# Zones of a one-core attention and MoE kernel, each 64 bytes longer

## The chip, the core and the metric

The kernel runs on one core of a Trainium2 chip. Its time is the device time of one execution in microseconds (us). Three runs of the kernel before took 904.09, 905.15 and 905.59 us; the median is 905.15 us. TensorE is the matrix engine (PE in the profile, PEld its loading of weights), VectorE is DVE, ScalarE is ACT, GpSimd is POOL, SyncE is SP. SBUF is the on-chip memory of 128 partitions that all operands are read from; PSUM holds the matmuls' results.

## The reference

Attention in four batches of eight heads, 576 positions, head size 64: half of the heads see a local window of 32 positions, half every 32nd position. Its output x (2304 tokens x 512) goes through two gated layers:

```
x = concat_heads(softmax(mask(q @ k.T / 8)) @ v)        # 2304 x 512
x = ((x @ w_a) * (x @ w_b)) @ w_out                     # 512 -> 1536 -> 512
y = (sigmoid(x @ w_gate) * (x @ w_val)) @ w_out2        # 512 -> 1536 -> 512
```

## The kernel before

Each fp32 product of the two layers is made of three passes over a high and a low part of both operands (high x high, low x high, high x low), in the type fp32r. The work has three stages.

**Stage one** (to about 502 us) holds the attention and the first layer. Tokens come in five tiles, four of 512 tokens and one of 256. For each tile and each of the 12 blocks k of 128 features, TensorE does 2 x 12 matmuls for the two factors (line 923, helper `product`) and 12 for the output of the block before (line 1013, `first_output`). The attention of the next tile is laid between these: the score products at line 563 (`qk`), the products with the values at line 618, transposes at lines 604 and 877. VectorE does the strided heads by multiplying and summing (lines 781 to 851).

**Stage two** (to about 770 us) is the gate and the value of the second layer, and **stage three** its output matrix. Both form block products with seven instead of eight multiplications: `seven` builds products whose matmuls, all at line 1292 (`prod`), have 384 columns. A product has 6 matmuls in stage two (two halves of the contraction, three passes) and 18 in stage three. Stage two runs 18 groups of two times 7 products, stage three 3 times two times 7. VectorE forms sums (`combine`, line 1133), splits operands (`split`, line 1144, with ScalarE at 1142) and merges results (lines 1304 and 1375).

The order of all work is made by a planner (`Plan`): each operation has an engine, a cost, a due time and the ranges of memory that it touches, and `run` issues the operation that can start first. Ranges are given in one flat address space in units of four bytes. It begins with 17 zones (`REGIONS`): 12 of 3072 elements (w0 to w11, 12288 bytes in each partition), four of 2048 (x12 to x15) and one of 1024 (h16). In stage one a w zone holds one block k's three weights in two parts, the x zones hold the tokens and h16 the features between the two products of the layer. In stages two and three the same zones hold tokens, weights, sums and their parts in other shares. What follows the zones (work buffers, raw weights, the ring of the attention) lies in one tile named `rest`.

The function `at(a, n, phase)` turns a flat range into a view of a tile. A zone's tile is made when the zone is first asked for in a phase, and all phases of a zone share one place in SBUF, since they have one tag:

```
if tiles.get(r, (None,))[0] != phase:
    name = f"{('w', 'x', 'h')[(r[0] >= X0) + (r[0] >= H0)]}{REGIONS.index(r)}"
    tiles[r] = phase, sb.tile([P, r[1]], F32, tag=name, name=f"{name}p{phase}")
v = tiles[r][1][:, a - r[0]:a - r[0] + n]
```

Tiles are laid behind each other in the order in which their tags are first used: the identity, the mask, `rest` (which begins at a multiple of 512 bytes), two small ones, then the zones w11, w10, w9, w7, w6, w8, w5, four small tiles of together 512 bytes, w4, x12, x14, x13, x15, w0, w1, h16, w2, w3. With "line" for a piece of 64 bytes, counted modulo 512 bytes (lines 0 to 7), every zone of the kernel before begins on line 6, and the 17 zones end at byte 228224 of a partition. Weights, tokens, features and their parts begin at multiples of 512 bytes from their zone's beginning: a block of weights is 128 columns of 4 bytes, a moving operand is 256, 384 or 512 such columns.

Of the kernel before, what the change touches and what calls it, by code (L numbers as in the profile page):

```python
# [7 lines left out]
F32 = mybir.dt.float32  # L8
# [14 lines left out]
P = 128  # L23
# [54 lines left out]
for _n, (_k, _w) in RINGS.items():  # L78
    if _n not in PLACE:
        PLACE[_n] = TOP  # L80
        TOP += _k * _w


def region_of(a):
    return next((r for r in REGIONS if r[0] <= a < r[0] + r[1]), None)
# [260 lines left out]
def attention_moe_kernel(ctx, tc, qkv, sq, sk, sv, w1, w2, mask, ident, out):  # L346
# [4 lines left out]
    sb = ctx.enter_context(tc.tile_pool(name="sb", bufs=1))  # L351
# [10 lines left out]
    tiles = {}  # L362

    def at(a, n, phase=FIRST, dtype=F32):
        r = region_of(a)
        if r is None:
            v = rest[:, a - F0:a - F0 + n]
        else:
            if tiles.get(r, (None,))[0] != phase:
                name = f"{('w', 'x', 'h')[(r[0] >= X0) + (r[0] >= H0)]}{REGIONS.index(r)}"  # L370
                tiles[r] = phase, sb.tile([P, r[1]], F32, tag=name, name=f"{name}p{phase}")
            v = tiles[r][1][:, a - r[0]:a - r[0] + n]
        return v if dtype == F32 else v.bitcast(dtype)

    def xT(i, c):

        return at(X0 + (2 * i + c // 2) * XZONE, XZONE, FIRST, F32R).rearrange("p (c n) -> p c n", c=HK)
# [5 lines left out]
    def buf(op, ring, shape, dtype=F32):  # L383
        s = op.slot[ring][0]
        if ring in PLACE:
            return at(PLACE[ring] + s * RINGS[ring][1], shape[1], FIRST, dtype)
        return sb.tile(shape, dtype, tag=f"{ring}{s}", name=f"{ring}{s}")
# [65 lines left out]
    def convert(w, need, start=()):  # L453
# [3 lines left out]
        def clear(op):  # L457
            for i in op.slot["c"]:
                tops.append(at(PLACE["c"] + i * DM, DM, FIRST, U32))
                POOL.memset(tops[-1], 0)  # L460
# [1133 lines left out]
```

## Time and profile before

| what | before |
|---|---|
| median of three runs | 905.15 us (904.09 to 905.59) |
| the profiled execution's own time | 903.51 us |
| its span, first to last instruction | 901.7 us |
| instructions in the profile | 13664 |
| TensorE busy | 893.2 us, 99% |
| VectorE, ScalarE, GpSimd busy | 654.9, 405.7, 11.7 us |

The profiled execution takes 1.8 us more than its span, and 1.6 us less than the median. The page gives the busy time of each engine, the chain of work that ended last, followed back from the last instruction, and the costliest groups of instructions; other views give the chain in order of time, the waits, stretches of time, or one line's instructions. A matmul's duration in the trace (334 ns for 384 columns) is longer than the distance to the next one's start, since matmuls are pipelined; what counts for the time is the distance, the pitch. It is read from the chain in order of time, where a piece gives its start, its length and the number of instructions in it.

### The profile page before, as it was taken

Reading aid. Unit: us, or ns where it says so; the run is one execution under the profiler, and the core shown is the slowest. Engines: PE = TensorE matmul, PEld = TensorE weight load, DVE = VectorE, ACT = ScalarE, POOL = GpSimd, SP = SyncE. Lnnn points to the kernel's source line nnn. Section 1 sums busy time; section 2 is a strip of 40 time slices with the busy share of each in tenths; the row PEclk is TensorE's granted clock in tenths of the full one; section 3 lists DMA queues with packets and bytes.
Section 4 is the critical chain, followed back from the end, with each engine's and each line's share of the span. In section 5 each row is a group of like instructions: output and inputs, shape, how many; then the busy total and the mean of one; then the engine's idle time right before and its main releaser. Section 6 shows DMA issues by size and latency. Waiting matters only on the chain.

```text
span 901.7 us, 13664 instructions
## 1 busy us (share of the span) xinstructions
PE 893.2 (99%) x5170; PEld 802.6 (89%) x5170; DVE 654.9 (73%) x1078; ACT 405.7 (45%) x843; POOL 11.7 (1%) x23
## 2 busy tenths in 40 slices
PE   8999999999999999999999999999999999999998
PEld 4678888888888888888899999999999999999998
DVE  7999988998999878811328876675768458649491
ACT  5775644411242113311236655564666445435351
POOL 4000000000000000000000000000000000000000
PEclk9999999999999999999999999999999999999999
DMA  9666564312332124300035243645574588953501
GB/s 311 203 232 219 201 201 135 91 44 63 92 128 72 54 65 144 96 1 1 0 118 164 94 139 113 216 152 187 200 243 168 196 306 331 378 166 116 167 17 62
DMA packets 62513, 132.67 MB, mean 147 GB/s; under 512 B 5872, under 2 KB 37232, under 8 KB 61552
## 3 DMA queue, kind: packets, MB, share of 16 engines
q1 hardware_dynamic: 62160, 131.60, 43.9%
q8 instruction: 40, 0.66, 0.3%
q10 hardware_dynamic: 288, 0.21, 0.1%
q14 instruction: 25, 0.20, 0.1%
HBM read 97.19 MB, written 34.60 MB: 146 GB/s over the span
## 4 chain that ended last, share of the span: by engine, by line
PE 96%; DVE 3%; DMA 0%; ACT 0%; issue 0%; DVEq 0%
PE bank L1292 43%; PE bank L923 32%; PE bank L1013 16%; PE idle L423 1%; PE bank L563 1%; PE bank L618 1%; PE bank L604 1%; DMA rest<-w 0%; PE bank L877 0%; DVE rest L491 0%; PE bank L436 0%; DVE w8p L851 0%; DVE w9p L851 0%; DVE nm L575 0%; DVE x14p L630 0%
## 5 line engine op out<-in xcount | busy, mean ns | idle before, releaser
L947 ACT CAST h16p<-rest 128x512 fp32r<-128x512 f32 (+1 forms) x60 | 34.7, 579 | 144.1 <-PE bank L1013 140.1
L1304 DVE TENSOR_TENSOR rest<-bank,rest 128x384 f32<-128x384 f32 x84 | 46.4, 555 | 57.3 <-PE bank L1292 32.5
L943 DVE TENSOR_TENSOR rest<-bank,rest 128x512 f32<-128x512 f32 (+1 forms) x60 | 38.1, 635 | 54.4 <-PE bank L923 54.1
L1065 ACT COPY rest<-bank 128x512 f32<-128x512 f32 (+1 forms) x60 | 32.7, 545 | 93.1 <-PE bank L923 91.6
L1310 ACT COPY rest<-bank 128x384 f32<-128x384 f32 x84 | 40.1, 479 | 67.2 <-PE bank L1292 66.9
L951 DVE TENSOR_TENSOR h16p<-rest,h16p 128x512 fp32r<-128x512 f32 (+1 forms) x60 | 38.2, 636 | 29.1 <-PE bank L1013 23.6
L781 DVE TENSOR_TENSOR rest<-rest 128x320 f32<-128x320 f32 (+13 forms) x56 | 51.5, 920 | 1.3 <-DMA rest<-sq 0.5
L844 DVE TENSOR_TENSOR rest<-rest,s 128x320 f32<-128x320 f32 (+13 forms) x56 | 51.5, 920 | 0.9
L787 DVE TENSOR_REDUCE s<-rest 128x5 f32<-128x320 f32 (+13 forms) x56 | 51.2, 914 | 1.2
L851 DVE TENSOR_REDUCE rest<-rest 128x64 f32<-128x320 f32 (+13 forms) x56 | 51.2, 914 | 1.0
L482 ACT ACTIVATE rest<-rest 128x512 f16<-128x512 bf16 x36 | 28.4, 793 | 9.2 <-DMA rest<-w 9.1
L1202 DVE SCALAR_TENSOR_TENSOR rest<-rest 128x512 uint32<-128x512 uint32 x36 | 24.7, 688 | 10.2 <-ACT rest L1195 10.2
L1195 ACT ACTIVATE rest<-rest 128x512 f16<-128x512 bf16 x36 | 28.0, 790 | 5.9 <-DMA rest<-w 5.8
L1375 DVE TENSOR_TENSOR rest<-bank,rest 128x384 f32<-128x384 f32 x36 | 20.0, 557 | 11.8 <-PE bank L1292 11.0
L1314 ACT COPY bank<-bank 128x384 f32<-128x384 f32 x42 | 19.6, 467 | 18.6 <-PE bank L1292 18.2
L1369 ACT ACTIVATE rest<-bank 128x384 f32<-128x384 f32 x36 | 17.8, 493 | 21.4 <-PE bank L1292 21.2
L491 DVE SCALAR_TENSOR_TENSOR rest<-rest 128x512 uint32<-128x512 uint32 x36 | 24.5, 684 | 0.9 <-ACT rest L482 0.9
L581 ACT ACTIVATE rest<-bank,nm 128x96 f32<-128x96 f32 x56 | 18.3, 339 | 12.2 <-DVE nm L576 10.6
L1369 ACT ACTIVATE rest<-rest 128x768 f32<-128x768 f32 x18 | 15.2, 846 | 14.2 <-DVE rest L1304 13.8
L1292 PE MATMUL bank<-w8p,w10p 128*128 128x384 f32 x100 | 20.7, 334 | 0.0
L1375 DVE TENSOR_TENSOR rest<-rest 128x768 f32<-128x768 f32 x18 | 17.2, 953 | 0.7 <-ACT rest L1369 0.2
L1292 PEld LDWEIGHTS bank<-w8p,w10p 128*128 128x128 f32 x100 | 17.6, 188 | 0.0
(500 smaller groups left out, 2413.8 us busy)
## 6 DMA issues: line engine op xcount, KB each, us to landing
rest<-w SPq DMA_DIRECT2D x72, 511.8 KB, 4.2
h2d<-rest SPq DMA_DIRECT2D x18, 768.0 KB, 4.2
rest<-qkv SPq DMA_DIRECT2D x12, 416.0 KB, 4.2
w2p<-h2d SPq DMA_DIRECT2D x12, 384.0 KB, 5.5
w0p<-h2d SPq DMA_DIRECT2D x12, 384.0 KB, 5.5
w1p<-h2d SPq DMA_DIRECT2D x12, 384.0 KB, 5.5
out<-rest SPq DMA_DIRECT2D x24, 192.0 KB, 1.8
x2d<-rest SPq DMA_DIRECT2D x16, 256.0 KB, 2.1
```

Of the source, the lines that this page charges most:

```text
L781: engine[op.eng].tensor_tensor(out=product(op, n), in0=x["k", h][:, :, :n, :], in1=x["q"][h // 2][:, e:e + nh, j:j + 1, :].to_broadcast([P ...
L787: DVE.tensor_reduce(out=weights_of(h, j, n), in_=x["p", op.deps[0]], op=ALU.add, axis=AX.X)
L844: engine[op.eng].tensor_tensor(out=product(op, n, "p (h d t) -> p h d t"), in0=x["v", h][:, :, :, :n], in1=weights_of(h, j, n).unsqueeze(2 ...
L851: DVE.tensor_reduce(out=xs[:, j, e:e + nh, :], in_=x["p", op.deps[0]], op=ALU.add, axis=AX.X)
L923: PE.matmul(x[tag][:, :n], ww[:, c * P:(c + 1) * P], xx(c), start=(u == 0 and c == chunks[0]), stop=(u == last and c == chunks[-1]),)
L943: DVE.tensor_tensor(out=x["g"], in0=x["b"][:, :n], in1=x["g"], op=ALU.mult)
L951: DVE.tensor_tensor(out=x["hl"], in0=x["g"], in1=r32(x["hh"]), op=ALU.subtract)
L1013: PE.matmul(ps[:, :n], ww[:, m * P:(m + 1) * P], x[xx], start=start, stop=stop)
L1292: PE.matmul(bank_of(where), at(*lhs(a, (0, 1, 0)[q], c), F32R), at(*rhs(b, (0, 0, 1)[q], c), F32R), start=p in OPENS and (q, c) == units[0 ...
L1304: DVE.tensor_tensor(out=at(*o), in0=bank_of("Z"), in1=at(*a), op=ALU.add)
L1310: "ACT", act2(NS), lambda op: ACT.copy(out=at(*o), in_=bank_of("Y")), [ops[after]], key - 20))
L1375: DVE.tensor_tensor(out=at(*o), in0=src(), in1=at(*o), op=ALU.mult)
```

## The change

Each zone's tile is 16 elements (64 bytes) longer, those of x12, x13 and x14 excepted. The views into the tiles stay as they were, at the tile's beginning. Since the tiles lie behind each other, each zone after a longer one begins 64 bytes further on; the zones end at byte 229120.

```
@@ -79,6 +79,9 @@
     if _n not in PLACE:
         PLACE[_n] = TOP
         TOP += _k * _w
+
+
+LINE, SAME = 16, ("x12", "x13", "x14")
 
 
 def region_of(a):
@@ -368,7 +371,7 @@
         else:
             if tiles.get(r, (None,))[0] != phase:
                 name = f"{('w', 'x', 'h')[(r[0] >= X0) + (r[0] >= H0)]}{REGIONS.index(r)}"
-                tiles[r] = phase, sb.tile([P, r[1]], F32, tag=name, name=f"{name}p{phase}")
+                tiles[r] = phase, sb.tile([P, r[1] + LINE * (name not in SAME)], F32, tag=name, name=f"{name}p{phase}")
             v = tiles[r][1][:, a - r[0]:a - r[0] + n]
         return v if dtype == F32 else v.bitcast(dtype)
```

## Rows read from the trace of the kernel before

**Rows 1.** The page: busy us and share of each engine; the granted clock in tenths

```profile
PE 893.2 (99%) x5170; PEld 802.6 (89%) x5170; DVE 654.9 (73%) x1078; ACT 405.7 (45%) x843; POOL 11.7 (1%) x23
...
PEclk9999999999999999999999999999999999999999
```

**Rows 2.** The page: the chain that ended last, shares by engine and by line

```profile
PE 96%; DVE 3%; DMA 0%; ACT 0%; issue 0%; DVEq 0%
PE bank L1292 43%; PE bank L923 32%; PE bank L1013 16%; PE idle L423 1%; PE bank L563 1%; PE bank L618 1%; PE bank L604 1%; DMA rest<-w 0%; PE bank L877 0%; DVE rest L491 0%; PE bank L436 0%; DVE w8p L851 0%; DVE w9p L851 0%; DVE nm L575 0%; DVE x14p L630 0%
```

**Rows 3.** Waits of TensorE: who waited for whom, us in total, times, longest

```profile
PE idle L423 <- DVE nil L421: 1.0, 1, 1.0
PE bank L877 <- DVE w9p L851: 0.8, 1, 0.8
PE bank L923 <- ACT x12p L627: 0.6, 1, 0.6
PE bank L1292 <- DVE w4p L1248: 0.6, 1, 0.6
```

**Rows 4.** The chain in order of time: start us, length us, what, how many

```profile
5.78 3.67 PE idle L423 x17
...
38.34 4.33 DMA rest<-w
...
106.85 2.72 PE bank L923 x12
...
458.22 2.88 PE bank L923 x24
...
503.58 43.69 PE bank L1292 x252
552.12 346.28 PE bank L1292 x1996
```

**Rows 5.** Stretches, line 1292 alone: PE and PEld busy (count), clock, DMA share, GB/s

```profile
720.00:740.00 20.00, 20.00 (x118) 20.00 (x117) 1.00 0.85 290
...
860.00:880.00 20.00, 20.00 (x117) 20.00 (x116) 1.00 0.03 11
```

**Rows 6.** The chain in order of time: the attention's score products at line 563

```profile
150.56 0.47 PE bank L563 x16
...
161.40 0.47 PE bank L563 x16
...
173.14 0.47 PE bank L563 x16
```

**Rows 7.** The chain in order of time: after transposes, and after 256-column matmuls

```profile
110.01 2.77 PE bank L923 x12
...
451.16 2.75 PE bank L1013 x12
```

**Rows 8.** Line 1292, 552.2 to 560 us: weight loads, duration ns min/median/max, starts

```profile
L1292 PEld LDWEIGHTS bank<-w1p,w10p x12: 188/188/188, 555.9 to 559.9; 128*128 128x128 f32 x12
...
L1292 PEld LDWEIGHTS bank<-w2p,w4p x10: 186/188/189, 552.1 to 554.7; 128*128 128x128 f32 x10
```

**Rows 9.** VectorE groups of 768 columns: count, busy us, mean ns, idle before

```profile
L1375 DVE TENSOR_TENSOR rest<-rest 128x768 f32<-128x768 f32 x18 | 17.2, 953 | 0.7 <-ACT rest L1369 0.2
...
L1133 DVE TENSOR_TENSOR rest<-w2p,rest 128x768 f32<-128x768 f32 x12 | 11.2, 950 | 0.0
L1133 DVE TENSOR_TENSOR rest<-w1p,w0p 128x768 f32<-128x768 f32 x9 | 8.4, 953 | 0.3 <-DMA w1p<-h2d 0.3
```

**Rows 10.** The page: DMA issues, KB each, median us to landing

```profile
rest<-qkv SPq DMA_DIRECT2D x12, 416.0 KB, 4.2
w2p<-h2d SPq DMA_DIRECT2D x12, 384.0 KB, 5.5
```

More of the change, by code (lines that the diff above doesn't have):

```diff
@@ L81 @@
         TOP += _k * _w
+LINE, SAME = 16, ("x12", "x13", "x14")
 def region_of(a):
@@ L370, in at @@
                 name = f"{('w', 'x', 'h')[(r[0] >= X0) + (r[0] >= H0)]}{REGIONS.index(r)}"
-                tiles[r] = phase, sb.tile([P, r[1]], F32, tag=name, name=f"{name}p{phase}")
+                tiles[r] = phase, sb.tile([P, r[1] + LINE * (name not in SAME)], F32, tag=name, name=f"{name}p{phase}")
             v = tiles[r][1][:, a - r[0]:a - r[0] + n]
```

## The prediction

> **What bounds the kernel now.** I read the profile from the outside in. The page's busy times [rows 1] show TensorE busy for 893.2 of 901.7 us at a granted clock of 1.0, that is 2.4 GHz, in all 40 slices; the reader should see that no other engine comes near it (VectorE 73%). Busy time alone does not say that TensorE sets the end, so the second view is the chain that ended last [rows 2]: 96% of it is TensorE, 43%, 32% and 16% in the lines 1292, 923 and 1013. The third is the table of waits [rows 3]: the longest single wait of TensorE is 1.0 us, at the start, and the largest totals are about 1 us. So from about 48 us to the end TensorE runs one matmul after the other, and the time is a count of matmuls times their pitch (start to start).
>
> The pitch is in the chain's long pieces [rows 4]. Twelve matmuls of 512 columns take 2.72 us, 226.7 ns each; 24 of 256 columns take 2.88 us, 120.0 ns; 252 and 1996 of 384 columns take 43.69 and 346.28 us, 173.4 and 173.5 ns. At 2.4 GHz the columns alone are 213.3, 106.7 and 160.0 ns. So **each of these matmuls costs 13.3 ns more than its columns**, the same for all three widths. The filling matmuls of line 423 (bf16, 512 columns) do better [rows 4]: 17 of them in 3.67 us, 215.9 ns, only 2.6 ns over their columns. The extra is steady: windows of 20 us [rows 5] hold 117 or 118 matmuls whether the DMA engines are busy 3% or 85%.
>
> How many there are follows from the code: stage one has, per group of 12 k and tile, 24 matmuls at line 923 and 12 at line 1013, in five tiles: 2160. Stage two has 18 groups of 14 products of 6 (1512), stage three 3 x 14 x 18 (756). Together 4428, and 4428 x 13.3 ns = 59 us of the span is this extra. Every one reads both its operands from zones, and every operand starts a multiple of 512 bytes into its zone; so in the kernel before all 4428 read weights and features from the same line (of eight lines of 64 bytes, modulo 512).
>
> **The change part by part.** It adds and removes no instruction, wait or DMA; no queue is passed by anything, and nothing is later in the order. The planner does not see the tile's size, so the schedule is the same. What moves is addresses, in three kinds of use.
>
> *TensorE.* Zones lie one behind the other in the order in which they are first used: w11, w10, w9, w7, w6, w8, w5, w4, x12, x14, x13, x15, w0, w1, h16, w2, w3. They all start on line 6 now. Afterwards the lines are 6, 7, 0, 1, 2, 3, 4, 5 for the weights up to w4, 6 for all four token zones, then 7, 0, 1, 2, 3. Of the 4428 matmuls 351 still read both operands from one line: 120 of line 923 (tokens with w11), 60 of line 1013 (h16 with w7), and 171 of line 1292, of which the pair of w3 with itself is 72. The other 4077 read two lines. The trace before has no such matmul of this kind, so I bound the effect on the pitch. Lower end: the extra falls from 13.3 to the fill's 2.6 ns [rows 4], a gain of 10.7 ns. Upper end: a loss of 4.2 ns, for which the nearest row is a stretch in which the pitch has not settled [rows 7]: after TensorE turned to transposes, 12 matmuls of 512 columns took 2.77 us and not 2.72, and after the change of width 2.75.
>
> I take **zero**. The row nearest to the question is the attention's score product at line 563 [rows 6]. It is no equal: fp32 in two passes, with 64 columns. But its weights are loaded beside the running matmul too, and its operands are cut at steps of 128 and 256 bytes, so that within one group of eight the keys start 0, 2, 4 and 6 lines ahead of the queries, each twice. The trace has two records per matmul; 16 records take 0.47 us, 58.8 ns for 2 x 64 columns (53.3 ns), in each of the three groups shown. If a common line cost 13 ns, the two matmuls in eight that have it would lift the group by 0.03 us over what the columns and the fill's 2.6 ns per pass make (8 x 58.5 = 0.47 us): there is no such room. The weight load says the same [rows 8]: a group whose first load ran on a waiting TensorE takes 186 to 189 ns, one whose loads all ran beside a matmul on the same line 188.
>
> The Trainium skill, page "TensorE: Matmul & The Clock Gate", section "Step-by-step: what each phase is for", has TensorE read the moving operand and the weights through two independent ports, so that loading the next weights takes nothing from the running matmul; by that the change is worth nothing and the sum stays. The same page's section "Back-to-back issue gap" gives N/2.4 + 2.5 ns, which the fill agrees with and the 384-column matmuls (162.5 by it, 173.5 measured) do not; by it the sum would be some 48 us less (4428 x 10.8 ns, an estimate), from a cause that it does not name.
>
> *VectorE and ScalarE.* Instructions whose two inputs lie on the same line and on different ones are both in the trace [rows 9]: 768 columns take 953 ns with both inputs in `rest` or both in zones, 950 ns with one in a zone and one in `rest`. That is 3 ns at most, and only 3% of the chain is VectorE [rows 2]: 27 us at 0.3% is 0.1 us. ScalarE has one input. Both are zero.
>
> *DMA.* The same packets go to starts shifted by multiples of 64 bytes. Transfers into zones (384 KB, 5.5 us) and into `rest`, which starts on line 0 (416 KB, 4.2 us), differ by what they collide with [rows 10]; no wait of TensorE in [rows 3] is for a transfer. The one long transfer on the chain, 4.33 us [rows 4], goes into `rest`, which does not move. Zero as well; the cover is that loads are issued ahead of their use, and if it were gone TensorE would wait for a transfer in stage three, where 384 KB take 5.5 us.
>
> The sum: 901.7 + 0 + 0.0 + 0 = 901.7 us of span, 903.5 us for the profiled execution, which is 1.6 us below the median of the runs, 905.15. So 905.2 us.
>
> **The rivals.** *The common line is what costs the 13.3 ns (faster).* For it: in all 4428 the next weights are read beside the running matmul and from the same line, nothing else in the trace explains the extra, and the pitch before it settles shows that it is no constant [rows 7]. Against it: [rows 6, 8, 9]. The price: 4077 x 10.7 ns = 43.6 us, 861.6 us; half of it, if two streams still meet once in each matmul at another place, 883.4 us.
>
> *The steady pitch is lost (slower).* Now the relation of the two streams never changes from matmul to matmul, and the pitch settles to 173.3 ns. With other lines it changes at some 530 places, 424 of them in line 1292 (about every fifth matmul there). If a change of line works as the change of width does in [rows 7], the matmuls between never settle: 4.2 ns on the 2268 of stages two and three is 9.5 us, 914.7 us; on all 4428 it is 18.6 us, 923.8 us. It decides wherever products alternate between zones faster than about ten matmuls; stage one, where the tokens share one line, would mostly escape. For it: [rows 7]. Against it: [rows 6], where lines change with each matmul and the pitch does not.
>
> *The change does not do what it says:* if the zones' starts were rounded to 512 bytes again, nothing would change, 905.2 us; that cannot be told from the forecast by the time.
>
> **How the numbers follow.** No effect has 0.45, the faster rival 0.36, the slower one 0.19. A measurement of this kernel can tell about 0.2% (1.8 us) from no change, and no effect stays within it. The first is likeliest: 905.2 us. The range takes in four fifths of the faster rival's full price (35 us: 870) and the slower one's price in stages two and three (915); the forecast's own range is 903.4 to 907.0. So faster 0.36, same 0.45, slower 0.19.
>
> **What would show it.** Right: the pieces of [rows 4] again at 226.7, 120.0 and 173.4 ns, and the same pitch for w3 with itself as for w8 with w10. The faster rival: pieces of line 1292 below 173 ns except for w3 with itself; the x12 pieces of line 923 below 2.72 us except those with w11. The slower one: pitches of line 1292 above 174 ns that vary, most where zones alternate. My step is wrong if the pitch of any of the three lines moves by over 0.5 ns.

## The result, and the profile after

The changed kernel took **913.16 us** (median of three runs, 912.42 to 914.15) against 905.15: a ratio of 1.0092, with a 95% interval of 1.0069 to 1.0115. It is slower by 8 us. That lies in the range given, but the likeliest case, no effect, did not come; the slower rival did, near its price of 914.7 us, and not where it was looked for. The profiled execution took 914.15 us, its span is 912.3 us. Line numbers are three higher than before: 1292 became 1295, 923 became 926, 1013 became 1016.

The page of the changed kernel, busy time, granted clock and the chain's shares, answers to [rows 1, 2]:

```profile
PE 903.0 (99%) x5170; PEld 805.3 (88%) x5170; DVE 655.2 (72%) x1078; ACT 405.1 (44%) x843; POOL 11.4 (1%) x23
...
PEclk9999999999999999999999999999999999999999
...
PE 95%; DMA 2%; DVE 1%; ACT 0%; SPq 0%; issue 0%; ACTq 0%
```

The instructions are as many as before, the clock is granted in full, VectorE and ScalarE are busy as long (654.9 and 405.7 us before), and only TensorE is busy longer, by 9.8 us. The DMA's 2% of the chain are the first 23 us, in which this execution began on another chain; no transfer is on it later.

The chain in order of time (start us, length us, what, how many), against [rows 4, 7]:

```profile
215.25 2.77 PE bank L1016 x12
218.02 5.58 PE bank L926 x24
223.60 2.80 PE bank L1016 x12
226.40 5.59 PE bank L926 x24
231.99 2.76 PE bank L1016 x12
...
470.47 2.73 PE bank L926 x24
473.20 1.42 PE bank L1016 x12
474.62 2.83 PE bank L926 x24
...
510.78 44.03 PE bank L1295 x252
...
559.68 349.33 PE bank L1295 x1996
```

Twelve matmuls of 512 columns, 2.72 us before, now take 2.76 to 2.80 us; 24 of 256 columns, 2.88 us before, take 2.73 to 2.83, so these became *faster*; the two long pieces of 384 columns are 0.34 and 3.05 us longer. The pitch varies from group to group now, in each width. The waits of TensorE [rows 3] (us in total, times, longest) stayed as short; those for transfers fall in the first 25 us:

```profile
PE idle L426 <- DVE nil L424: 1.0, 1, 1.0
PE bank L926 <- ACT x12p L630: 0.6, 1, 0.6
PE bank L1295 <- DVE w4p L1251: 0.6, 1, 0.6
PE bank L566 <- DMA w5p<-qkv: 0.6, 1, 0.6
PE bank L566 <- DMA w7p<-qkv: 0.6, 1, 0.6
```

The score products in the chain in order of time [rows 6] take what they took:

```profile
153.97 0.47 PE bank L566 x16
164.86 0.47 PE bank L566 x16
176.83 0.47 PE bank L566 x16
```

Nor did the weight loads' own durations change [rows 8] (ns, shortest, median and longest):

```profile
L1295 PEld LDWEIGHTS bank<-w2p,w4p x10: 187/188/190, 559.7 to 562.2; 128*128 128x128 f32 x10
```

Nor VectorE's instructions of 768 columns [rows 9] (busy us, mean ns):

```profile
L1378 DVE TENSOR_TENSOR rest<-rest 128x768 f32<-128x768 f32 x18 | 17.1, 952 | 0.4
...
L1136 DVE TENSOR_TENSOR rest<-w2p,rest 128x768 f32<-128x768 f32 x12 | 11.2, 950 | 0.0
```

A steadier measure than any piece is the sum of the distances from each matmul's start to the next instruction's on TensorE, over all matmuls of a line and width. It is worked out from the starts in each kernel's trace, and the table has it for every kernel of this study (us; "over before" is the sum of the four less 847.34):

| kernel | 512 columns, L923 | 512, L1013 | 256, both lines | 384, L1292 | over before |
|---|---|---|---|---|---|
| before | 268.36 | 132.06 | 52.09 | 394.83 | |
| after | 272.35 | 134.49 | 51.25 | 398.23 | +9.0 |
| e1_apart4 | 268.26 | 132.06 | 52.10 | 394.83 | -0.1 |
| e2_apart3 | 274.61 | 133.22 | 50.39 | 395.27 | +6.2 |
| e3_shift_all | 268.39 | 132.12 | 52.10 | 394.85 | +0.1 |
| e4_scan16 | 273.37 | 135.07 | 51.37 | 399.13 | +11.6 |
| e5_sets2 | 269.90 | 133.09 | 51.93 | 399.20 | +6.8 |
| e6_sets4 | 268.35 | 132.08 | 52.10 | 394.92 | +0.1 |
| e7_last48 | 268.31 | 132.03 | 51.14 | 394.83 | -1.0 |
| e8_all17 | 272.08 | 134.69 | 51.23 | 398.37 | +9.0 |
| e9_alt01 | 272.54 | 134.39 | 51.37 | 398.46 | +9.4 |
| e10_tok48 | 268.21 | 132.03 | 50.39 | 394.80 | -1.9 |
| e11_alt04 | 268.27 | 132.06 | 52.09 | 394.81 | -0.1 |

Where nothing happens the sum comes back within 0.1 us. So the 9.0 us of the changed kernel are no scatter: 4.0 + 2.4 us are matmuls of 512 columns, 3.4 us those of 384, and 0.8 us are given back by 256 columns. That covers the loss (the medians differ by 8.0 us, and their interval goes from 6.2 to 10.4). The two profiled spans differ by 10.6 us; the other 1.6 us lie almost wholly before the first matmul of the layer, which starts 25.4 us in and not 23.9. That start moves from 23.8 to 26.4 us among the kernels of this study, also where no pitch changed (25.0 us in e6 and e11).

### The profile page after: what moved, and what is told of

Read it like the earlier page. It is cut to its first block, busy times and chain, and to the rows that moved or that the text cites. A ratio compares the mean times of both kernels' runs of the same rounds, so it can differ in the third digit from the quotient of the medians.

```text
span 912.3 us, 13664 instructions
## 1 busy us (share of the span) xinstructions
PE 903.0 (99%) x5170; PEld 805.3 (88%) x5170; DVE 655.2 (72%) x1078; ACT 405.1 (44%) x843; POOL 11.4 (1%) x23
## 4 chain that ended last, share of the span: by engine, by line
PE 95%; DMA 2%; DVE 1%; ACT 0%; SPq 0%; issue 0%; ACTq 0%
PE bank L1295 43%; PE bank L926 33%; PE bank L1016 17%; PE bank L621 1%; DMA rest<-w 1%; PE bank L566 1%; DMA w6p<-qkv 1%; DMA w9p<-sv 1%; PE bank L607 1%; PE bank L880 0%; DVE rest L494 0%; DVE w0p L506 0%; DVE w4p L1251 0%; DVE rest L1307 0%; ACT w4p L1248 0%
## 5 line engine op out<-in xcount | busy, mean ns | idle before, releaser
L1295 PE MATMUL bank<-x15p,w3p 128*128 128x384 f32 x88 | 17.6, 336 | 0.0
```

The lines of the kernel that those rows point to most:

```text
L1295: PE.matmul(bank_of(where), at(*lhs(a, (0, 1, 0)[q], c), F32R), at(*rhs(b, (0, 0, 1)[q], c), F32R), start=p in OPENS and (q, c) == units[0 ...
```

## The experiments

"Distance" below is the line at which a matmul's moving operand starts less the line of its weights, where a line is 64 bytes. Three theories stood at the start. **A**: the distance sets the pitch, and only modulo four lines (256 bytes). **B**: any constant distance is good; what costs is a change of distance, after which the pitch has to settle again. **C**: what matters is a common line modulo 512 bytes. Sorting the changed kernel's steady stretches of 512 columns by distance modulo four had given 226.7, 228.9, 232.6 and 233.3 ns for zero to three lines. In the edits, `MORE` holds the elements (16 to a line) by which a zone's tile is longer than before; zones behind it move.

**Four lines, three lines, all together, and a scan.** The first kernel puts the token zones four lines off all weights, the second three lines, so that stage one has a constant distance there. The third lengthens `rest` by one line, so that all zones move together. The fourth puts the weight zones on different multiples of 16 bytes.

```
 e1  MORE = {"w4": 64, "x15": 64}
 e2  MORE = {"w4": 48, "x15": 80}
-    tiles[r] = phase, sb.tile([P, r[1]], F32, tag=name, ...)
+    tiles[r] = phase, sb.tile([P, r[1] + MORE.get(name, 0)], F32, tag=name, ...)
 e3
-    rest = sb.tile([P, TOP - F0], F32, name="rest")
+    rest = sb.tile([P, TOP - F0 + 16], F32, name="rest")
 e4  AT: each zone's shift in pieces of 16 bytes; odd ones by a later start of the view
+AT = dict(zip(ORDER17, (1, 2, 3, 5, 6, 7, 9, 10, 16, 16, 16, 16, 27, 29, 32, 46, 47)))
+FRONT = {z: s % 2 * 4 for z, s in AT.items()}
+            a += FRONT[...]        (by the zone's name; MORE makes up the rest of the shift)
```

> The four token zones alone begin 4 lines (256 bytes) further on; all other zones share one line. Theory A (the pitch of a matmul is set by the distance of its moving operand from its weights modulo 256 bytes): 256 bytes count as none, 226.7 ns at line 923 and 173.3 ns at line 1292, the time of before within 1 us. Theory B (any distance is good once it stays; changes of distance cost): the distance stays for 24 matmuls and flips between tokens and h16, so 227 to 229 ns at line 923, 1 to 3 us over before. Theory C (a common line modulo 512 bytes matters, as the change supposes): line 923 reads two lines and line 1013 one, so the two differ by several ns from each other and the time moves by 4 us or more.

> The same with 3 lines (192 bytes). Theory A: 233.3 ns at line 923 with 512 columns (226.7 before) and 115.7 ns with 256 (120.0 before), line 1013 stays at 226.7 and 120.0 ns; 6 to 8 us over before. Theory B: the same as with 4 lines, 227 to 229 ns and 1 to 3 us over before. Theory C: the same as with 4 lines.

> The tile in front of the zones is 64 bytes longer, so all zones move by one line together and their distances stay. Theories A, B and C: the pitches of before, 226.7, 120.0 and 173.3 ns, and the time of before within 1 us. If the line itself mattered, or the distance of the zones from the tile named rest, it would show here alone.

> Each zone of weights has another distance from the tokens and h16, in steps of 16 bytes (all multiples of 16 from 0 to 240 but 0, 64, 128 and 192). Theory A: line 923 has another steady pitch for each, between 226.7 and 233.3 ns with 512 columns, changing smoothly or by lines of 64 bytes; 4 to 12 us over before. Theory B: the distance stays for 24 matmuls within one block, so all blocks have the same pitch, 227 to 229 ns. Theory C: 15 of 16 distances cross lines in part, the pitches fall into two groups.

Four lines: 904.22 us, ratio 0.9998 (0.9988 to 1.0008), and every pitch as before. C falls: a distance of four lines is as good as none. Moving all zones together: 904.84 us, 1.001 (1.000 to 1.0021); one line further on for all of them leaves every pitch as it was; what counts is how the zones stand to each other. Three lines: 910.35 us, 1.0065 (1.0045 to 1.0086), the 6 to 8 us of A. Its chain in order of time, in a stretch of 512 columns and at the end of 256 columns:

```profile
217.78 5.60 PE bank L926 x24
223.38 2.74 PE bank L1016 x12
226.12 5.60 PE bank L926 x24
...
462.22 2.83 PE bank L926 x24
...
466.48 2.74 PE bank L926 x24
469.22 1.42 PE bank L1016 x12
470.64 2.74 PE bank L926 x24
```

At a constant three lines 24 matmuls of 512 columns take 5.60 us, 233.3 ns each, in every group, where the kernel before has 5.44 (226.7); line 1016, whose features stay at zero lines, has 2.74 (228) with its first matmuls after each turn unsettled. So for 512 columns B falls as the whole cause: a distance that never changes within a piece costs 6.6 ns. For 256 columns the same distance *gains*: 2.74 us for 24, 114 ns, against 120.0, where line 1016 before it also has 256 columns; the group at 462.22 us, which follows line 1016 with 512 columns, takes 2.83 us, 118 ns. For 384 columns the constant distances zero, one and three of this kernel all settled at 173.3 to 173.6 ns. The scan took 914.99 us, from one run alone; for 512 columns zero was better than any of the 12 other distances in steps of 16 bytes (226.7 ns in the kernel before; means of settled stretches from 227.3 to 234.3 ns), so no hidden better place was found there.

**Two sets of zones, two lines and four lines apart.** For 384 columns A and B were still open. Here w10, w5 and w4 stand off all others: the distance is two lines in 1620 of 2268 matmuls, but rarely changes.

```
 e5  MORE = {"w11": 32, "w10": 32, "w8": 32, "w4": 32}
 e6  MORE = {"w11": 64, "w10": 64, "w8": 64, "w4": 64}
```

> The zones w10, w5 and w4 alone lie two lines (modulo four) off all other zones. In stages two and three the two streams are then two lines apart in 1620 of the 2268 matmuls of 384 columns, but the distance changes at only 47 places, against 368 in the changed kernel. In stage one 432 matmuls of 512 columns and 108 of 256 columns read at that distance. Both theories expect stage one to lose 432 x 5.9 = 2.5 us and to gain 108 x 1.2 = 0.1 us there. Theory A (the distance itself sets the pitch of 384 columns too, 176 ns at two lines): line 1292 gains 1620 x 2.6 = 4.2 us, pitch 176 ns wherever the distance is two lines, the whole 6.7 us over the kernel before, ratio 1.007. Theory B for 384 columns (any constant distance settles at 173.3 ns, each change of distance costs some 9 ns, 3.4 us by 368 changes): 47 changes cost 0.4 us, pitch 173.3 ns, the whole 2.9 us over the kernel before, ratio 1.003.

> The same four tiles longer as in the kernel with two sets of zones, but by twice as much: w10, w5 and w4 lie four lines off all others. Theories A and B with a period of 256 bytes: every matmul reads at a distance of zero lines modulo four, no distance changes, so no change: 904 to 906 us, ratio 1.000. A period of 512 bytes (four lines are then a distance of their own, and the places where it changes cost): about the loss of the kernel with two sets, 1.003 to 1.007.

Two lines: 910.70 us, 1.0073 (1.0059 to 1.0087), 6.6 us over before where A had 6.7; line 1295 has +4.4 us, where A had 4.2 and B 0.4. The chain in order of time, a stretch at two lines and one at zero:

```profile
520.88 12.67 PE bank L1295 x72
...
798.95 18.20 PE bank L1295 x105
```

72 matmuls at a constant two lines take 176.0 ns each to the end of the piece, 105 at zero 173.3 in the same kernel. The distance counts for 384 columns too. Four lines: 904.33 us, 1.0003 (0.9993 to 1.0013): the 256 bytes again.

**All 17 zones longer.** The three token zones that the change leaves out are longer as well. Distances stay spread as they were, but stage one now changes between them some 750 times and not some 80.

```
-LINE, SAME = 16, ("x12", "x13", "x14")
+LINE = 16
-    ... r[1] + LINE * (name not in SAME)
+    ... r[1] + LINE
```

> All 17 zones are 64 bytes longer, so the token zones x12 to x15 begin on four lines too. In stage one the places where the distance changes become 751 (512 and 256 columns) and not 78 as in the changed kernel, while the counts of matmuls at each distance stay nearly as they were. Theory A (the distance itself counts in stage one): by the pitches at each distance the sum is 8.3 us over the kernel before, against 8.6 for the changed kernel, so as the changed kernel within 0.5 us, about 913 us. Theory B (changes cost, about 9 ns each, in stage one as in the others): some 670 more changes cost about 6 us more than the changed kernel, about 919 us.

912.80 us, 1.0096 (1.0077 to 1.0114): as A had it, and not the 919 of B. But A was right here for a wrong reason. By its table a distance of zero gives 226.7 ns; in this trace the matmuls of 512 columns with that distance have a mean of 231.5 ns, and those with three lines 231.2 (pitches over 300 ns, 15 of each, left out; by the same count the changed kernel has 228.8 and 232.9). Where neighbours change, the distance no longer sorts the pitch: the good one is lost, and the bad one gets a little better.

**Changes alone.** Seven zones lie one line off the others. The distance is zero, one or three lines, all of which had settled at 173.3 ns with 384 columns, but changes there at 369 places, as often as in the changed kernel. Its counterpart has four lines in place of one (and w0 in place of w1), 335 places.

```
 e9   MORE = {"w7": 16, "x12": 48, "x13": 16, "x15": 48, "w0": 16, "w1": 48}
 e11  MORE = {"w7": 64, "x12": 64, "x13": 64, "w0": 64}
```

> The zones w6, w8, w5, w4, x12, x15 and w1 lie one line (modulo four) off all others, so the two streams are zero, one or three lines apart and never two. In the lines of 384 columns the distance changes at 369 places, as often as in the changed kernel (368). Where the distance stays, zero, one and three lines all settled at 173.3 ns so far. Theory A (the distance alone): line 1292 stays at 394.8 us. Theory A with B (a distance of two lines costs 2.8 ns each, and every change costs some ns more, whatever the distances: of the changed kernel's 3.4 us in this line 1.4 us are its 587 matmuls at two lines, and the other 2.0 us are 368 changes at 5.4 ns): line 1292 gains 2.0 us. In stage one 336 and 480 matmuls of 512 columns lie one and three lines apart: by the settled pitches 0.7 + 3.2 us more, and 0.7 us less from 204 matmuls of 256 columns. The whole: 3.2 us over the kernel before by A, 5.2 us by A with B, ratio 1.0035 or 1.0058.

> The zones w6, w8, w5, w4, x12, x15 and w0 lie four lines (256 bytes) off all others, so the two streams are zero or four lines apart, about half of the 4428 matmuls each, and the distance changes between these two at 335 places in the lines of 384 columns, 431 in those of 512 and 107 in those of 256. Modulo 256 bytes nothing changes anywhere. Theory A with B and a period of 256 bytes: nothing happens, 226.7, 120.0 and 173.3 ns as before, ratio 1.000. A change of line as such costs (whatever the period of the distance), as it did with zones one line apart: line 1292 gains about 335 x 9.8 = 3.3 us, the 512 columns about as much again, ratio 1.006 to 1.009. The planned order and everything else stay as they were.

One line: 913.52 us, 1.0091 (1.0073 to 1.0109), above both expectations. Line 1295 has +3.6 us; A alone had none and A with B 2.0. Stage one lost 5.8 us by the table, where the settled pitches gave 3.2. So changes do cost here, 3.6 us / 369 = 9.8 ns each; that is the mean of this mix, for 108 changes in the kernel with the token zones three lines on cost line 1295 0.4 us, 4 ns each. How they do is seen in two stretches of line 1295 in this kernel, in both of which the two operands start three lines apart modulo four (the moving one on line 6 or 2 and the weights on line 7; in the first two matmuls of the second stretch on lines 6 and 3). The pair of w9 with w4 is in both:

```profile
541.01 7.42 PE bank L1295 x42
...
865.84 6.59 PE bank L1295 x38
```

The starts of the trace give these distances from matmul to matmul, in ns, once each had settled:

```
541 us:  177 176 178 175 178 176 177 176 178 175 178 176   (mean 176.7 over 42)
866 us:  174 173 173 174 173 173 174 173 173 174 173 173   (mean 173.3 over 38)
```

Neither drifts towards the other within some 40 matmuls. **One distance has more than one steady pitch, and which of them a stretch gets depends on what it came from.** The second half is argued here; the last two kernels below show it for 256 columns. So a change of distance does not merely cost a few matmuls of settling; it can leave the whole stretch behind it in the worse one. With four lines in place of one, as many changes cost nothing: 905.32 us, 1.0009 (0.9997 to 1.002), each line within 0.1 us of before. A change of line as such is free; a change modulo 256 bytes is not.

**What 256 columns gain.** The last token tile alone, and in the first version its features too, start three lines later within their zones; nothing else moves. The start of the tokens is written in three places, one of which is shown.

```
+def start_of(i):
+    return i % 2 * N2 + 48 * (i == NJ - 1)
...
-        o = (i % 2) * N2
+        o = start_of(i)
 e7 alone
+        o = 48 * (n < N2)
-            x["hh"] = buf(op, "hh", [P, N2], F32R)[:, :n]
+            x["hh"] = buf(op, "hh", [P, N2], F32R)[:, o:o + n]
```

> The kernel before, with nothing moved but the last token tile of stage one (256 columns) and the parts of its features: they begin 48 elements, three lines, later in their zones and buffers. All 432 matmuls of 256 columns then read at a distance of three lines. Theory A: their pitch falls from 120.0 to 114.1 to 115.7 ns, 432 x 4.3 to 5.9 = 1.9 to 2.5 us less, ratio 0.9972 to 0.998, faster than both kernels. Theory B (any constant distance is as good as zero): 120.0 ns, ratio 1.000. Nothing else moves: 226.7 and 173.4 ns in the other lines.

> As the kernel with the last token tile and its features three lines on, but only the tokens: the features stay where they were. The 288 matmuls of 256 columns in line 923 then read three lines apart, the 144 of line 1013 at zero, as in the kernel with the token zones three lines on, where line 923 settled at 113.3 ns after line 1013's zero distance. Theory A (the distance alone): line 923 falls to 118 ns as it did with both moved, 0.6 us less, line 1013 stays, ratio 0.9993. Theory A with B (the pitch also hangs on what the stream came from): 113.3 to 115 ns settled, 288 x 5 = 1.4 us less, and up to 0.2 us less in line 1013: 1.4 to 1.7 us less, ratio 0.9982, faster than both kernels.

Both moved: 902.93 us, 0.9983 (0.9974 to 0.9993); the lines give 1.0 us, half of what was expected. Tokens alone: **902.30 us, 0.9973 (0.9960 to 0.9986)**, 1.9 us by the lines, faster than both kernels of the case. Of these 1.7 us are matmuls of 256 columns: A with B had 1.4 to 1.7, A alone 0.6. The chain in order of time, first with both moved, then with the tokens alone:

```profile
461.46 1.41 PE bank L1019 x12
462.88 2.83 PE bank L928 x24
465.70 1.41 PE bank L1019 x12
467.12 2.83 PE bank L928 x24
```

```profile
461.14 1.42 PE bank L1018 x12
462.56 2.74 PE bank L928 x24
465.30 1.42 PE bank L1018 x12
466.72 2.74 PE bank L928 x24
```

The tokens' matmuls of line 928 have the same distance in both, and 2.83 us for 24 in the one, 2.74 in the other: 118 ns against 113.3 settled. With both at three lines the stretch keeps the pitch that it came with; the turn from zero lines (line 1018) to three throws it into the better one. That is the finding of the kernel with changes alone once more, here to the kernel's good.

## Why the prediction was right or wrong

**TensorE, "I take zero": this step failed.** The pitches were to stay within 0.5 ns. By the table 1728 matmuls of 512 columns lost 3.7 ns each (6.4 us), 2268 of 384 columns 1.5 ns (3.4 us), and 432 of 256 columns gained 1.9 ns (0.8 us). The row chosen as nearest, the score products [rows 6], was read rightly and was no measure. Their operands have distances of zero and two lines modulo four alone, which change from matmul to matmul; within a group the pitch is 57 to 60 ns at both. A distance that lasts, and one of one or three lines, does not occur among them. That 16 records of line 566 take 0.47 us after the change too says nothing more, for queries and keys of these groups lie in one buffer in `rest` and were not moved against each other. Whether fp32 in two passes reacts to a lasting distance was not tried; the fp32r matmuls do react. The weight load's duration [rows 8] was no measure either: it is 187 to 190 ns after the change while the pitch is longer. The prediction had seen that the width and the unsettled stretches move the pitch [rows 7], and that the extra of 13.3 ns is unexplained; an extra of 59 us in the very matmuls whose operands move, with no cause known, should have outweighed a row of another type.

The Trainium skill, page "TensorE: Matmul & The Clock Gate", section "Step-by-step: what each phase is for", with its two independent ports and a weight load that takes nothing from the running matmul, gave the same zero. For these fp32r matmuls the trace does not agree with that zero: with moving operand and weights a constant 192 bytes apart a matmul of 512 columns takes 233.3 ns, with none 226.7. The runs don't show whether it is the reading of the two operands that collides.

**Bounds of that step.** Its upper end of +4.2 ns was too low for 512 columns, where a settled stretch costs up to 6.6 ns, and it is about right for 384 columns, where 2.7 ns are lost at two lines and 3.3 in the worse of two steady pitches. The lower end, a gain of 10.7 ns, came nowhere; the largest gain is 6.7 ns, for 256 columns.

**The faster rival fell** for 3996 of the 4428 matmuls: a common line is not what costs there, it is the best of all distances tried for 512 columns, and as good as any constant one for 384. For the 432 of 256 columns it had the right sign: there another distance, three lines, gave back up to 6.7 of the 13.3 ns. The 13.3 ns remain in the kernel before with every operand on one line, and what they are is still open.

**The slower rival came, with a wrong address.** It had 9.5 us in stages two and three and let stage one "mostly escape", since its tokens share one line. Stages two and three lost 3.4 us and stage one 5.6 (6.4 less 0.8). What the rival had right is that a steady pitch is lost where the distance changes: 369 changes alone cost line 1295 3.6 us. What it lacked is that the distance itself sets a pitch, so a stage with few changes loses as well: with tokens at a constant three lines, line 923 lost 6.3 us (274.61 against 268.36). And its period was wrong: modulo 512 bytes 352 of the matmuls still had a common line by the trace (351 in the prediction); modulo 256 there are 924, and all of the effect goes by that. That its price agreed with the result was luck: two errors, one up and one down, nearly cancelled.

**The changed kernel's 3.4 us of 384 columns** cannot be parted cleanly: by its trace the 587 matmuls at two lines are 2.4 ns above before (1.4 us) and the others, at distances that are harmless when constant, make the other 2.0 us; changes alone made 3.6 us in another mix.

**VectorE, ScalarE, DMA: zero, right.** 952 and 950 ns for 768 columns, the same waits of TensorE, and no transfer on the chain after the start. That the change does not do what it says is answered by the pitches.

**The numbers.** 913.2 us is within the range of 870 to 915, near an end that was taken from the rival's smaller price, and not by the step that the forecast of 905.2 us stood on; the chance of 0.19 for it was low, because the one row that spoke against it was taken for more than it showed.

## What to carry to other kernels

In a stream of fp32r matmuls the starts of the moving operand and of the weights modulo 256 bytes belong to the layout: keep them equal for 512 columns (three lines, though constant, cost 6.6 ns each), equal or at one constant distance of one or three lines through a long run for 384, and measure other distances for narrow ones (three lines made 256 columns 2 to 6% faster). A padding that seems free should be a multiple of 256 bytes here. Judge such a thing by the start-to-start distances of the very instructions, in their own type and width; the row of another type here had neither lasting nor odd distances and said little.

## What the runs showed of the hardware that was not expected

- The pitch of an fp32r matmul depends on where its two operands start relative to each other, with a period of 256 bytes. In settled stretches: 512 columns 226.7, 228.9, 232.6 and 233.3 ns at zero to three lines; 384 columns 173.3 at constant zero, one and three, 176.0 at two; 256 columns 120.0 at zero, 113.3 or 118 at three. Moving both operands together changes nothing (e3), nor do four lines (e1, e6, e11). Whether the running matmul's own weights count or those that are loaded beside it was not tried; in long stretches both have the same distance.
- The stream can hold several steady pitches at one distance: 173.3 and 176.7 ns (384 columns, three lines), 113.3 and 118 ns (256 columns, three lines). What came before decides (e7 against e10, where the matmuls of line 928 read the same addresses), and some 40 matmuls don't undo it (e9).
- None of it shows in the busy time's share, the waits, the clock or a load's duration: TensorE is 99% busy before and after. It is seen in the start-to-start distance alone.
